# Softmax denominators of two attention pairs in one group of matrix products, in the first phase of a QK-norm attention and squared-ReLU kernel

## The chip, the cores and the metric

One core of one Trainium2 chip runs the whole program. The metric is device time in microseconds (us) from the first to the last instruction of the core with what lies around it; lower is better. All data are 32-bit floats. The engines are TensorE (PE, with its weight loads shown as PEld), VectorE (DVE), ScalarE (ACT), GpSimd (POOL) and SyncE (SP), which issues nearly all transfers.

## The reference

```
rmsnorm(x, g) = x / sqrt(mean(x*x) + 1e-6) * g
q_n, k_n = rmsnorm(q, g_q), rmsnorm(k, g_k)      # (8, 12, 448, 64): batch, heads, sequence, head size
attn = softmax(q_n @ k_n^T / sqrt(64))
a = attn @ v                                     # (8, 12, 448, 64)
x = a, heads side by side                        # (3584, 768)
out = relu(x @ w_in)^2 @ w_out                   # w_in 768 x 2048, w_out 2048 x 768
```

## The kernel before

Heads are worked on in *pairs*: pair `i` is two heads (`e` = 0, 1) of one batch, so 128 rows of "head element" on the partitions; there are 8 x 6 = 48. The 448 keys of a head are three blocks of 128 (`m` = 0, 1, 2) and 64 last ones (`m` = `NJ` = 3). The last keys of an even pair and of the odd pair behind it share one tile of 128 rows.

*Phase 1* is what the change touches: pairs 0 to 11 (`alone(i)`: the first two batches), before any of the second half's products exist to be mixed in. The instructions are in a hand-written order (a manual schedule): each engine works through its own in program order, and waits where data or a buffer isn't there. The loop makes 13 visits, each of two halves (`visit_alone(i, n)`). In visit `i`:

- `n = 0`: `weigh_slots` forms the scores of pair `i`, key blocks 0 and 1 (`score`: L449, 64x64 stationary tiles, four in different quarters of the array; PSUM banks 0 to 3), and ACT takes their exponentials (`weigh`, L468) into `weights`. `turn(i + 1, x)` transposes q (x = 0) and k (x = 1) of the next pair on PE (L415, L418; banks 7 and 6); DVE copies q and multiplies it by the gains (L423), ACT copies k (L425). `square(i + 2, x)` squares q on ACT (L181) and k on POOL (L183). `begin(step)` does pieces of a conversion of the second half's weights (ACT L1696 to L1699, DVE L1710, L1729, DVE or POOL L1810). `normalize(i + 2, 0)` sums the squares on DVE (L194, L197), raises them to -1/2 on POOL (L204), and scales q on POOL (L219). The factor for k goes into the exponential. Then `attend(i - 1)` multiplies the exponentials of the pair before by the values, blocks 0 to 2 (L552; `values_bank`: bank 4 for even pairs, 5 for odd ones).
- `n = 1`: scores and exponentials of block 2, in even visits also of the last keys of pairs `i` and `i + 1` (L460); `normalize(i + 2, 1)`; in odd visits `attend_both(i - 1)`, the last keys' values of two pairs (L588; the odd pair's part to bank 6, from where ACT copies it to `rest`, L595). Then for pair `i - 1`: `add_weights`, the denominators (L604): eight products of `ones` with the exponentials, each giving 32 equal rows in one of four column groups; `take_sums`, a DVE transpose in 32x32 blocks (L664); `invert`: four small copies (L675), an addition (L676), a reciprocal (L681) and a transpose that spreads the result again (L682); `finish`: DVE multiplies the values by the inverse (L717; for odd pairs after adding `rest`, L715). From the second batch on, `begin_forms` subtracts finished pairs from one another (L744): for its first three pairs one subtraction on DVE, for the last three one on DVE and two on POOL.

The buffers for `weights` are rooms in tiles named `part`, `acc` and `wT`.

After visit 12 the second half begins with L1016. It is mixed with the attention of the later pairs, whose denominators come in another way: POOL adds the exponentials up (L487), and one product for each head (L622) finishes the sum. For pair 12 that runs right behind phase 1.

The core of the order around the change:

```
            weigh_slots(i, n)
            turn(i + 1, 0)
            turn(i + 1, 1)
...
                attend(i - 1, (NJ,))
                add_weights(i - 1, range(NJ + 1))
                forget(i - 1, range(NJ + 1))
                take_sums(i - 1)
                invert(i - 1)
                finish(i - 1)
```

Of the kernel before, what the change touches and what calls it, by code (L numbers as in the profile page):

```python
# [14 lines left out]
F32 = mybir.dt.float32  # L15
# [4 lines left out]
ALU = mybir.AluOpType  # L20
# [3 lines left out]
P = 128  # L24


NJ = 3
NG = 2 * NJ + 1
SIDE = 32
# [196 lines left out]
def program(ctx, tc, rows, v, g, wide, ones, moe_w_in, moe_w_out, out, shift):  # L226

    nc = tc.nc

    B, H, S, D = v.shape  # L230
    NPAIR = H // 2
# [6 lines left out]
    NT = S // P  # L238
# [23 lines left out]
    banks = [psum.tile([P, 512], F32, name=f"bank{n}") for n in range(8)]  # L262
# [36 lines left out]
    def key_of(i, m):  # L299
        return (i - i % 2, m) if m == NJ and not shift else (i, m)  # L300

    def alone(i):

        return pairs[i][0] < 2
# [104 lines left out]
    def turn(i, x):  # L409

        ensure("qk", i)
        tr = banks[7 - x if i < 2 or alone(i - 2) else 0]
        dst = att.tile([P, S], F32, name="qT" if x == 0 else "kT")
        for j in range(NJ):
            nc.tensor.transpose(  # L415
                tr[:, ts(j, P)], rows.part(i, x)[:, j].rearrange("p h d -> p (h d)"), ident
            )
        nc.tensor.transpose(  # L418
            tr[:, ts(NJ, P)], rows.room(i)[:, x, NJ].rearrange("p h d -> p (h d)"),
            wide[:, ds(i % 2 * LASTS, P)],  # L420
        )
        if x == 0:
            nc.vector.tensor_scalar(out=dst, in0=tr[:, 0:S], scalar1=g, scalar2=None, op0=ALU.mult)  # L423
        else:
            nc.scalar.copy(dst, tr[:, 0:S])  # L425
        turned[i, x] = dst

    def new_weights(n, e):

        i, m = n  # L430
        if m < 2 and alone(i) and not shift:
            weights[n, e] = new_acc()[:, 0:S] if m else new_part()
        else:
            weights[n, e] = att.tile([P, S], F32, name="wT", tag="wT", bufs=8)
        return weights[n, e]

    def banks_of(i, m):

# [90 lines left out]
    def values_bank(i):  # L529
        return banks[4 + i % 2 if alone(i) else 4][:, 0:S]  # L530

    def attend(i, some):

        order = values_of(i)
        for n in (i, i + 1 if i % 2 == 0 and not shift else i):
            ensure("v", n)
        for n in some:  # L540
            if n >= len(order):
                continue
            m = order[n]
            if m == NJ and not shift:
                attend_both(i)
                continue
            if joint(i):
                attend_halves(i, n)
                continue
            mine = ds(i % 2 * LASTS, LASTS) if m == NJ else ds(0, P)  # L550
            for e in range(2):
                nc.tensor.matmul(  # L552
                    values_bank(i)[ds(e * D, D), :],
                    lhsT=lasts[i % 2][mine, e, :] if m == NJ else values[i][:, m, e, :],
                    rhs=weights[key_of(i, m), e][mine], start=n == 0,
                    stop=n == len(order) - 1 and (shift or i % 2 == 1),
                )

    def second_bank(i):
        return banks[3][:, 0:S]  # L560
# [36 lines left out]
    def add_weights(i, some):  # L597

        order = sums_of(i)
        for n in some:  # L600
            m = order[n]
            mine = ds(i % 2 * LASTS, LASTS) if m == NJ and shift else ds(0, P)
            for e in range(2):
                nc.tensor.matmul(  # L604
                    sums_bank(i)[ds(e * D + n % 2 * SIDE, SIDE), :],
                    lhsT=ones_of[i % 2][mine] if m == NJ else ones[:, 0:SIDE],
                    rhs=weights[key_of(i, m), e][mine], start=n < 2, stop=n >= 2,
                )
# [53 lines left out]
    def take_sums(i):  # L662
        inverse[i] = io.tile([P, S], F32, name="inverse", tag="squares", bufs=1)
        nc.vector.transpose(inverse[i], sums_bank(i))  # L664
# [4 lines left out]
    def invert(i):  # L669
        columns = inverse[i].rearrange("p (t n) -> p t n", n=SIDE)  # L670
        few = columns[:, :, 0:1]
        if alone(i) or shift:
            other, both = new_few(), new_few()
            for n in range(P // SIDE):
                nc.vector.tensor_copy(out=other[ts(n, SIDE)], in_=few[ts(n ^ 1, SIDE)])  # L675
            nc.vector.tensor_tensor(out=both, in0=few, in1=other, op=ALU.add)  # L676
            few = both
        if shift:
            nc.vector.tensor_scalar(out=few, in0=few, scalar1=1e-9, scalar2=None, op0=ALU.add)
        by = new_few()  # L680
        nc.vector.reciprocal(out=by, in_=few)  # L681
        nc.vector.transpose(columns, by.to_broadcast([P, S // SIDE, SIDE]))  # L682
# [22 lines left out]
    def finish(i):  # L705

        b, c = pairs[i]
        if joint(i):
            xT = xts[b, c]
            nc.gpsimd.tensor_tensor(out=xT, in0=xT, in1=inverse.pop(i), op=ALU.mult)  # L710
        else:
            xT = xts[b, c] = new_x()
            bank = values_bank(i)
            if i % 2 and not shift:
                nc.vector.tensor_tensor(out=xT, in0=bank, in1=rests.pop(i), op=ALU.add)  # L715
                bank = xT
            nc.vector.tensor_tensor(out=xT, in0=bank, in1=inverse.pop(i), op=ALU.mult)  # L717
        leave(i)

    def leave(i):  # L720
        b, c = pairs[i]
        scale_turned()
        for x in range(2):
            del turned[i, x]
        del values[i]
        if b == 1:
            begin_forms(c)
        elif b > 1:
            settle(b, c)
# [1129 lines left out]
    load_weights(1)  # L1859
    for i in range(2, 4):  # L1860
        rows.load(i, nc.sync)
    for n in range(2):
        nc.gpsimd.memset(ones_of[n][ds((1 - n) * LASTS, LASTS)], 0.0)
        nc.gpsimd.memset(ones_of[n][ds(n * LASTS, LASTS)], 1.0)

# [83 lines left out]
    def new_acc():  # L1949
        return keep_p.tile([P, DM], F32, name="acc", tag="acc", bufs=2 * NT + 1)  # L1950
# [30 lines left out]
    def visit_alone(i, n):  # L1981
        step = i * 2 * VISITS + 2 * n
        if n == 0:
            if i == 0:
                load_v(i)
            if i and shift:
                attend_all(i - 1)
            weigh_slots(i, n)
            turn(i + 1, 0)
            turn(i + 1, 1)  # L1990
            square(i + 2, 0, new_acc())
            square(i + 2, 1, new_acc(), nc.gpsimd)
            begin(step)
            normalize(i + 2, 0)
            if i and not shift:
                attend(i - 1, range(NJ))
        else:
            weigh_slots(i, n)
            normalize(i + 2, 1)
            begin(step)  # L2000
            if in_blocks(i + 2):
                store_q(i + 2)
                load_blocks(i + 2, 0)
                load_blocks(i + 2, 1)
            if i and not shift:
                attend(i - 1, (NJ,))
                add_weights(i - 1, range(NJ + 1))
                forget(i - 1, range(NJ + 1))
                take_sums(i - 1)
                invert(i - 1)  # L2010
                finish(i - 1)
            if i < 2 * NPAIR:
# [196 lines left out]
```

## Time and profile before

| | |
|---|---|
| runs | 1348.09, 1348.0, 1348.48; median 1348.09 us |
| profiled execution | 1348.26 us, its span 1346.5 us |
| granted TensorE clock | 0.999 |
| busy, share of the span | PE 98%, PEld 66%, DVE 66%, ACT 45%, POOL 56% |
| the profile's stretch of phase 1 | some 0 to 122 us |

The profile is one execution. "Busy" counts the time in which an engine works at something; matrix products are pipelined, so a busy PE can still be a PE that gains from fewer products. Each product of 32-bit floats stands as two instructions in the trace, so the eight products of a pair's denominators are L604 x16. Rows give line, engine, operation, tiles written and read, and shapes; a bracket at the end tells how long the engine stood idle before and what released it. The chain of waits follows the work that ended last back to its releasers.

### The profile page before, as it was taken

To read this page: it belongs to the slowest core of one execution; us is meant where nothing else is said; L and a number is where in the kernel's file an instruction comes from. 1 tells how busy PE (TensorE), PEld (TensorE's weight loads), DVE (VectorE), ACT (ScalarE), POOL (GpSimd) and SP (SyncE) were. 2 spreads that over 40 slices of the span, in tenths; PEclk is the share of its full clock that TensorE was granted. 3 is DMA by queue.
4 is the path that set the end of the run, shared out by engine and by line. 5 is a ranking of instruction groups with operands and counts; after the bars stand their busy time and mean duration, and the time that the engine had idled before them with its cause. 6 is when DMAs were issued, how large, how long until landed. Compare 5 with 4: busy or idle time off the path is not lost.

```text
span 1346.5 us, 21086 instructions
## 1 busy us (share of the span) xinstructions
PE 1326.0 (98%) x6988; PEld 887.2 (66%) x6988; DVE 884.0 (66%) x1739; ACT 611.4 (45%) x1135; POOL 760.6 (56%) x740
## 2 busy tenths in 40 slices
PE   7999999999999999999999999999999999999998
PEld 3333454444444486777758576676858599999998
DVE  4887866878768856465656856565655854556673
ACT  6885677768666244442434244353433134330000
POOL 5668764746556878566767878576555731110010
PEclk9999999999999999999999999999999999999999
DMA  5655965968969877574748676674737466545543
GB/s 137 156 142 131 247 187 144 283 182 219 266 149 268 255 189 221 154 219 124 234 104 251 190 186 211 169 214 119 238 83 231 145 194 196 157 132 152 161 158 101
DMA packets 416633, 245.64 MB, mean 182 GB/s; under 512 B 273284, under 2 KB 381060, under 8 KB 415492
## 3 DMA queue, kind: packets, MB, share of 16 engines
q1 hardware_dynamic: 416224, 244.15, 64.2%
q8 instruction: 57, 0.93, 0.3%
q14 instruction: 60, 0.49, 0.1%
q10 hardware_dynamic: 292, 0.07, 0.0%
HBM read 178.13 MB, written 65.99 MB: 181 GB/s over the span
## 4 chain that ended last, share of the span: by engine, by line
PE 90%; DVE 4%; DMA 2%; SPq 1%; POOL 1%; issue 1%; ACT 1%; POOLq 0%; DVEq 0%; ACTq 0%
PE bank L1077 26%; PE bank L1274 21%; PE bank L1600 9%; PE bank L1016 8%; PE bank L449 8%; PE bank L567 4%; PE bank L552 4%; PE bank L1438 2%; PE bank L460 1%; PE bank L588 1%; PE bank L604 1%; PE bank L1216 1%; PE bank L631 1%; PE bank L622 1%; DVE acc L1636 1%
## 5 line engine op out<-in xcount | busy, mean ns | idle before, releaser
L1077 PE MATMUL bank<-xT,in_sb 128*128 128x224 f32 x1344 | 287.0, 353 | 0.0
L1077 PEld LDWEIGHTS bank<-xT,in_sb 128*128 128x128 f32 x1344 | 253.1, 190 | 9.4 <-ACT wT L468 5.6
L468 ACT ACTIVATE wT<-bank,rr 128x448 f32<-128x448 f32 x288 | 163.8, 631 | 160.5 <-PE bank L449 134.9
L1274 PE MATMUL bank<-out_sb,hid 128*128 128x384 f32 x576 | 206.0, 490 | 1.7 <-DVE acc L1636 1.6
L204 POOL TENSOR_TENSOR rr<-ms,minus_half 128x8 f32<-128x8 f32 (+1 forms) x96 | 145.9, 1520 | 75.4 <-DVE ms L197 70.4
L1636 DVE TENSOR_TENSOR acc<-acc,bank 128x384 f32<-128x384 f32 x231 | 122.3, 546 | 78.7 <-PE bank L1274 58.6
L1274 PEld LDWEIGHTS bank<-out_sb,hid 128*128 128x128 f32 x576 | 107.7, 190 | 81.6 <-issue 6.6
L1274 PE MATMUL bank<-out_sb,sums 128*128 128x384 f32 x432 | 155.7, 491 | 1.1 <-DVE acc L1636 0.6
L449 PE MATMUL bank<-qT,kT 64*64 64x448 f32 x1152 | 147.0, 553 | 1.9 <-DVE qT L423 1.1
L1016 PE MATMUL bank<-xT,in_sb 128*128 128x448 f32 x336 | 129.8, 543 | 0.0
L1274 PEld LDWEIGHTS bank<-out_sb,sums 128*128 128x128 f32 x432 | 80.5, 190 | 65.5 <-issue 4.2
L487 POOL TENSOR_TENSOR sum<-sum,wT 128x448 f32<-128x448 f32 (+1 forms) x96 | 116.4, 1233 | 1.6
L1016 PEld LDWEIGHTS bank<-xT,in_sb 128*128 128x128 f32 x336 | 62.8, 190 | 66.8 <-issue 63.0
L1060 DVE TENSOR_TENSOR hid<-hid,bank 128x224 f32<-128x224 f32 x208 | 73.4, 382 | 44.3 <-PE bank L1077 41.1
L449 PEld LDWEIGHTS bank<-qT,kT 64*64 64x64 f32 x1152 | 49.5, 134 | 76.2 <-issue 50.8
L487 POOL TENSOR_TENSOR sum<-wT 128x448 f32<-128x448 f32 x48 | 56.1, 1189 | 73.1 <-ACT wT L468 66.5
L1077 PE MATMUL bank<-more,in_sb 128*128 128x224 f32 x288 | 74.4, 354 | 0.0
L567 PE MATMUL bank<-wT,vt 64*64 64x448 f32 x576 | 74.4, 545 | 0.0
L382 ACT ACTIVATE qT<-qT,g 128x448 f32<-128x448 f32 x34 | 22.5, 663 | 106.6 <-DVE qT L372 106.6
L1699 ACT ACTIVATE words<-words 128x384 f16<-128x384 f32 x64 | 68.6, 1072 | 2.0
L1547 POOL TENSOR_TENSOR acc<-acc 128x768 f32<-128x768 f32 x2 | 4.3, 2138 | 105.3 <-DVE acc L1519 105.3
L1060 DVE TENSOR_TENSOR whole_hid<-whole_hid,bank 128x224 f32<-128x224 f32 x104 | 37.7, 385 | 39.1 <-PE bank L1077 37.1
(200 smaller groups left out, 2374.7 us busy)
## 6 DMA issues: line engine op xcount, KB each, us to landing
in_sb<-in_deep SPq DMA_DIRECT2D x64, 384.0 KB, 3.8
in_sb<-in_deep SPq DMA_DIRECT2D x80, 256.0 KB, 4.3
out_sb<-out_forms SPq DMA_DIRECT2D x48, 384.0 KB, 5.6
words<-in_moe_w_in_dram SPq DMA_DIRECT2D x32, 384.0 KB, 3.9
words<-in_moe_w_out_dram SPq DMA_DIRECT2D x32, 384.0 KB, 3.5
out_forms<-out_sb SPq DMA_DIRECT2D x8, 1536.0 KB, 7.0
qk<-in_q_dram SPq DMA_DIRECT2D x96, 96.0 KB, 2.6
qk<-in_k_dram SPq DMA_DIRECT2D x96, 96.0 KB, 2.7
```

The lines of the kernel that those rows point to most:

```text
L204: self.nc.gpsimd.tensor_tensor(out=self.rr[i][:, x, 0 : self.count(i)], in0=ms, in1=self.minus_half.to_broadcast(list(ms.shape)), op=ALU.pow,)
L449: nc.tensor.matmul(sc[ds(half * D, D)], lhsT=turned[i, 1][ds(e * D, D), ds(m * P + half * D, D)], rhs=turned[i, 0][ds(e * D, D), :], start ...
L468: nc.scalar.activation(new_weights((i, m), e), sc, AF.Exp, scale=rows.rr[i][:, 1, 2 * m + e : 2 * m + e + 1],)
L487: nc.gpsimd.tensor_tensor(out=sums[i, e][some], in0=left[some], in1=weights[key_of(i, m), e][some], op=ALU.add)
L567: nc.tensor.matmul(bank[ds(e * D, D), :], lhsT=values[i][keys, n, e, :], rhs=weights[(i, n), e][keys], start=n == 0, stop=n == NJ - 1 and ...
L1016: nc.tensor.matmul(ps, lhsT=w_sb[:, IN.index(left), c, :], rhs=forms[u, c][right], start=first and c == 0, stop=c == NK - 1, skip_group_ch ...
L1060: nc.vector.tensor_tensor(out=quarter(blk, name, n), in0=quarter(blk, base, n), in1=ps, op=ALU.add)
L1077: nc.tensor.matmul(ps, lhsT=left, rhs=right, start=start, stop=stop, skip_group_check=True)
L1274: nc.tensor.matmul(ps, lhsT=lefts[left][:, t, ts(tt, P)], rhs=w_sb[t][:, OUT.index(right), :], start=first and t == 0, stop=t == 1, skip_g ...
L1600: nc.tensor.matmul(ps, lhsT=left[l][:, blk], rhs=rest_of[r][:, blk], start=blk == 0 and product in ("P1", "P5", "P4"), stop=blk == NBLK - ...
L1636: nc.vector.tensor_tensor(out=acc, in0=acc, in1=ps, op=ALU.add)
L1699: nc.scalar.activation(sign, high.bitcast(F32), AF.Copy)
```

## The change

- *Denominators of two pairs in one group.* Odd visits no longer form any. In even visits (2, 4, ... 12) `sums_of_two(i - 2)` forms those of pairs `i - 2` and `i - 1`: six products for each pair, with a stationary operand whose ones stand in 16 of 32 columns (the first 16 for the even pair, the other 16 for the odd one), and two for the shared last keys, each split in two products of 224 columns so that all four column groups work. All go to bank 6.
- *Inversion.* One transpose out of the bank, four small copies, an addition and a reciprocal serve both pairs (`invert_two`); two transposes spread the results.
- *Values.* In odd visits `leave_bank(i - 1)` copies the even pair's values from bank 4 to its `xT`, and `finish` later multiplies them there. In even visits both pairs are finished, one after the other.
- *Order of the turn.* In odd visits from 3 on, `turn(i + 1, 1)`, then `turn(i + 1, 0)`, stand ahead of the scores; k's transposes then use bank 4 instead of 6.
- *Rooms.* Exponentials live longer, so some go to tiles of the second half that are unused in phase 1 (`new_spare`); the masks with 16 columns of ones lie there too.

```
+    def turned_first(i):
+        return i % 2 == 0 and 2 < i <= 2 * NPAIR and not shift
...
-        tr = banks[7 - x if i < 2 or alone(i - 2) else 0]
+        tr = banks[4 if x and turned_first(i) else 7 - x if i < 2 or alone(i - 2) else 0]
...
+    def new_spare():
...
+        half = SIDE // 2
+        masks = more[:, 6 * S // SIDE : 6 * S // SIDE + 5 * half]
+        nc.gpsimd.memset(masks, 0.0)
+        nc.gpsimd.memset(masks[:, ts(1, half)], 1.0)
+        for n in range(2):
+            nc.gpsimd.memset(masks[ds(n * LASTS, LASTS), ts(3 + n, half)], 1.0)
+        spare.append([masks[:, ds(n * half, SIDE)] for n in (1, 0, 3)])
+
+    def room_for_weights(i, m, e):
+        if i % 4 == 0 or i == 2 * NPAIR - 1:
+            return spare[2 * m + e]
+        if m == 0:
+            return new_part()
+        if i % 2 == 0:
+            return spare[4 + 2 * m + e]
+        if m == 1:
+            return new_acc()[:, 0:S]
+        return att.tile([P, S], F32, name="wT", tag="wT", bufs=8)
...
+    def sums_of_two(i):
+        bank = banks[6][:, 0:S]
+        ones_for = spare[14]
+        for n in range(2 * NJ + 1):
+            p, m = divmod(n, NJ) if n < 2 * NJ else (0, NJ)
+            for e in range(2):
+                some = weights.pop(((i + p, m), e))
+                if m < NJ:
+                    nc.tensor.matmul(
+                        bank[ds(e * D + n % 2 * SIDE, SIDE), :], lhsT=ones_for[p], rhs=some,
+                        start=n < 2, stop=False, skip_group_check=True,
+                    )
+                    continue
+                for half in range(2):
+                    columns = ts(half, S // 2)
+                    nc.tensor.matmul(
+                        bank[ds(e * D + half * SIDE, SIDE), columns], lhsT=ones_for[2],
+                        rhs=some[:, columns], start=False, stop=True, skip_group_check=True,
+                    )
+        inverse[i] = io.tile([P, S], F32, name="inverse", tag="squares", bufs=1)
+        nc.vector.transpose(inverse[i], bank)
+        inverse[i + 1] = spare[10]
+
+    def invert_two(i):
+        columns = [inverse[i + p].rearrange("p (t n) -> p t n", n=SIDE) for p in range(2)]
+        few = columns[0][:, :, 0 : SIDE : SIDE // 2]
+        other, both, by = spare[11:14]
+        for n in range(P // SIDE):
+            nc.vector.tensor_copy(out=other[ts(n, SIDE)], in_=few[ts(n ^ 1, SIDE)])
+        nc.vector.tensor_tensor(out=both, in0=few, in1=other, op=ALU.add)
+        nc.vector.reciprocal(out=by, in_=both)
+        for p in range(2):
+            nc.vector.transpose(
+                columns[p], by[:, :, p : p + 1].to_broadcast([P, S // SIDE, SIDE])
+            )
+
+    def leave_bank(i):
+        xT = xts[pairs[i]] = new_x()
+        nc.vector.tensor_copy(out=xT, in_=values_bank(i))
+        del values[i]
...
+        elif (b, c) in xts:
+            xT = xts[b, c]
+            nc.vector.tensor_tensor(out=xT, in0=xT, in1=inverse.pop(i), op=ALU.mult)
...
-            weigh_slots(i, n)
-            turn(i + 1, 0)
-            turn(i + 1, 1)
+            if turned_first(i + 1):
+                turn(i + 1, 1)
+                turn(i + 1, 0)
+                weigh_slots(i, n)
+            else:
+                weigh_slots(i, n)
+                turn(i + 1, 0)
+                turn(i + 1, 1)
...
-            if i and not shift:
+            if i % 2 and not shift:
                 attend(i - 1, (NJ,))
-                add_weights(i - 1, range(NJ + 1))
-                forget(i - 1, range(NJ + 1))
-                take_sums(i - 1)
-                invert(i - 1)
+                leave_bank(i - 1)
+            elif i and not shift:
+                sums_of_two(i - 2)
+                invert_two(i - 2)
+                finish(i - 2)
                 finish(i - 1)
```

More of the change, by code (lines that the diff above doesn't have):

```diff
@@ L430, in new_weights @@
         i, m = n
-        if m < 2 and alone(i) and not shift:
-            weights[n, e] = new_acc()[:, 0:S] if m else new_part()
+        if m < NJ and alone(i) and not shift:
+            weights[n, e] = room_for_weights(i, m, e)
+        elif m == 1 and i == 2 * NPAIR and not shift:
+            weights[n, e] = new_acc()[:, 0:S]
         else:
@@ L435, in new_weights @@
         return weights[n, e]
+    spare = []
+    def new_spare():
+        for a in range(2):
+            some = hidden_p.tile([P, 2, 2, S], F32, name="hid", tag=f"hid{a}", bufs=1)
+            spare.extend(some[:, n // 2, n % 2] for n in range(4))
+        some = [
+            hidden_p.tile([P, 2, NT * P], F32, name="sums", tag=f"S{n}", bufs=1).rearrange(
+                "p t n -> p (t n)"
+            ) for n in range(3)
+        ]
+        spare.extend(x[:, 0:S] for x in some)
+        more = some[2][:, S : 2 * NT * P]
+        for n in range(3):
+            spare.append(more[:, ts(n, 2 * S // SIDE)].rearrange("p (t n) -> p t n", n=2))
+        half = SIDE // 2
[15 more added lines that the diff above has]
+        return att.tile([P, S], F32, name="wT", tag="wT", bufs=8)
     def banks_of(i, m):
@@ L724, in leave @@
             del turned[i, x]
-        del values[i]
+        values.pop(i, None)
         if b == 1:
@@ L1861, in program @@
         rows.load(i, nc.sync)
-    for n in range(2):
+    if not shift:
+        new_spare()
+    for n in range(2 if shift else 0):
         nc.gpsimd.memset(ones_of[n][ds((1 - n) * LASTS, LASTS)], 0.0)
@@ L2004, in visit_alone @@
                 load_blocks(i + 2, 1)
-            if i and not shift:
+            if i % 2 and not shift:
                 attend(i - 1, (NJ,))
-                add_weights(i - 1, range(NJ + 1))
-                forget(i - 1, range(NJ + 1))
-                take_sums(i - 1)
-                invert(i - 1)
+                leave_bank(i - 1)
[3 more added lines that the diff above has]
+                finish(i - 2)
                 finish(i - 1)
+                if i == 2 * NPAIR:
+                    spare.clear()
             if i < 2 * NPAIR:
```

## Prediction

> **What bounds the kernel now.** I read the page's totals first, then the chain of waits in order of time over phase 1 (the part that the change touches), then the timelines of PE, DVE, POOL and ACT over the same stretch, and last the busy time by pairs of visits.
>
> ```profile
> span 1346.5 us, 21086 instructions
> PE 1326.0 (98%) x6988; PEld 887.2 (66%) x6988; DVE 884.0 (66%) x1739; ACT 611.4 (45%) x1135; POOL 760.6 (56%) x740
> ```
>
> TensorE (PE) bounds the whole. Its share is an average, so phase 1 is read from its own chain. This is visit 3; columns are start, length, what:
>
> ```profile
> 36.56 1.66 PE bank L449 x16
> 38.22 0.48 PE bank L415 x3
> 38.70 0.11 PE bank L418
> 38.81 0.33 PE bank L415 x3
> 39.14 0.11 PE bank L418
> 39.25 2.40 PE bank L552 x12
> 41.65 0.91 PE bank L449 x8
> 42.56 0.75 PE bank L588 x8
> 43.32 1.64 PE bank L604 x16
> ```
>
> It ends at 44.96, 8.40 us without a gap: scores of key blocks 0 and 1 (1.66), the transposes of the next pair (0.48 + 0.11 + 0.33 + 0.11 = 1.03), the value products (2.40), scores of block 2 (0.91), the last keys (0.75; in even visits these are scores, L460), the denominators (1.64). L449 with 8 instructions takes 0.91 behind products of another shape; L588, also 8, takes 0.75 behind the same 64x64 shape. So a change of shape costs 0.16. Two visits, odd then even, take 16.8 while PE is the only limit. Here each window begins where an even visit's denominators end; the columns are length, then busy time of PE, PEld, DVE, ACT, POOL:
>
> ```profile
> 36.56:53.36 16.80, 16.80 (x140) 6.15 (x143) 14.73 (x37) 13.93 (x26) 9.69 (x8) 1.00 0.64 159
> 53.36:70.16 16.80, 16.80 (x140) 6.15 (x143) 14.25 (x34) 15.25 (x29) 10.50 (x9) 1.00 0.55 139
> 70.16:87.14 16.98, 16.98 (x140) 6.32 (x142) 15.76 (x38) 15.14 (x28) 11.99 (x11) 1.00 0.62 146
> 87.14:103.87 16.73, 16.73 (x137) 6.24 (x136) 14.59 (x35) 13.82 (x25) 8.78 (x8) 1.00 0.52 121
> 103.87:122.29 18.42, 17.01 (x141) 6.22 (x137) 15.97 (x33) 8.69 (x17) 15.85 (x14) 1.00 0.61 177
> ```
>
> Together 85.73. DVE is busy for 85 to 94% of the first four windows. It isn't the bound by its sum, but it works in program order, and one loop through it comes close. The denominators reach DVE, which inverts and divides; only behind that in its queue stand the qT copy of the next pair and the row sums (L194) of the pair after that; POOL raises those to a power (L204) and scales q by them (L219); the next visit's transposes need the scaled q. Visit 5, DVE and then POOL:
>
> ```profile
> 53.45 0.65 DVE L664 STREAM_TRANSPOSE inverse<-bank 128x448 f32<-128x448 f32 x1
> 54.13 1.67 DVE L675 COPY few<-inverse 32x14 f32<-32x14 f32 x4
> ...
> 56.32 0.65 DVE L682 STREAM_TRANSPOSE inverse<-few 128x448 f32<-128x448 f32 x1
> ...
> 57.51 0.77 DVE L717 TENSOR_TENSOR xT<-xT,inverse 128x448 f32<-128x448 f32 x1
> 58.20 0.67 DVE L423 TENSOR_SCALAR qT<-bank,g 128x448 f32<-128x448 f32 x1
> 58.80 0.54 DVE L194 TENSOR_REDUCE ms<-acc 128x6 f32<-128x384 f32 x1
> ...
> 59.62 1.36 POOL L204 TENSOR_TENSOR rr<-ms,minus_half 128x6 f32<-128x6 f32 x1 [1.83 <-DVE ms L197]
> 61.06 0.83 POOL L219 TENSOR_TENSOR qk<-qk,rr 128x384 f32<-128x384 f32 x1
> ```
>
> The loop ends at 61.89, 8.53 after the denominators (53.36). The transposes want it at 53.36 + 8.40 + 1.66 = 63.42. The other four odd visits, and the place where it fails already:
>
> ```profile
> 44.80 0.83 POOL L219 TENSOR_TENSOR qk<-qk,rr 128x384 f32<-128x384 f32 x1
> ...
> 79.00 0.95 POOL L219 TENSOR_TENSOR qk<-qk,rr 128x384 f32<-128x384 f32 x1
> ...
> 94.44 0.83 POOL L219 TENSOR_TENSOR qk<-qk,rr 128x384 f32<-128x384 f32 x1
> ...
> 114.60 0.83 POOL L219 TENSOR_TENSOR qk<-qk,rr 128x384 f32<-128x384 f32 x1
> 115.49 0.55 PE L415 MATMUL bank<-wide,qk 128*128 128x128 f32 x3 [0.96 <-POOL qk L219]
> ```
>
> Counted from the window's start, the loop ends at 9.07, 8.53, 9.79, 8.13 and 11.56, against a need at 10.06. It has 0.27 to 1.93 to spare, and in visit 12 PE stands 0.96 for it.
>
> **The change, part by part.** *Denominators.* Two groups (3.28) in two visits become one. Twelve products are as wide as now: 24 instructions, four at a time in four column groups, so 6 waves; a wave now takes (1.64 - 0.16)/4 = 0.37. Four products are half as wide. Their price is bounded by the full wave (0.37) and by half of it; the nearest row is of 224 columns:
>
> ```profile
> L1077 PE MATMUL bank<-xT,in_sb 128*128 128x224 f32 x1344 | 287.0, 353 | 0.0
> ```
>
> 287.0/1344 = 0.21, so a half wave is near 0.2; two of them. 6 x 0.37 + 0.4 + 0.16 = 2.76 (3.1 at the upper bound). Saved: 0.52 in two visits. Odd visits now end in 64x64 products and the next begins with such: one change of shape less, 0.16.
>
> *Order of the turn.* In odd visits transposes stand before the scores instead of behind them: the same shapes in turn, no PE time. k goes first, q second, so q is wanted 0.59 into the visit. Its loop started in an even visit, whose predecessor no longer inverts anything, so it is early: nothing. No transfer moves (q and k are loaded two visits ahead; the turn issues none). ACT's kT copy passes ahead of four exponentials which wait for later scores anyway: nothing.
>
> *No denominators in odd visits.* They covered the exponentials of block 2, which empty banks 0 and 1 before the next visit's scores write them. An odd visit is now 1.03 + 1.66 + 2.40 + 0.91 + 0.75 = 6.75. The exponentials end like this (visit 3):
>
> ```profile
> 42.60 1.16 ACT L468 ACTIVATE wT<-bank,rr 128x448 f32<-128x448 f32 x2
> ```
>
> 43.76 is 7.20 into the window: the new wait is 0.45, up to 1.0 where ACT converts words first, 0 where it doesn't. I take 0.5.
>
> *DVE.* One inversion for two pairs drops four copies, an addition, a reciprocal, and one 0.65 transpose out of a bank in two visits; a copy of the even pair's bank to xT is added in odd visits (L717's 0.6 as its price), where DVE waits for PE before its next transpose anyway. What counts is order: an even visit's denominators are now followed by both inverse transposes and both finishes. The stretch ahead of qT and L194 grows by one L682 (0.65) and one multiplication (0.6): 1.25. Behind visit 8's group one more subtraction for the forms joins it, behind visit 10's too; these rows are its price, and the late start of DVE in visit 10 as it is now:
>
> ```profile
> L744 DVE TENSOR_TENSOR xT<-xT x6: 624/624/626, 83.2 to 127.0; 128x448 f32<-128x448 f32 x6
> 105.02 0.64 DVE L664 STREAM_TRANSPOSE inverse<-bank 128x448 f32<-128x448 f32 x1
> ```
>
> *Sum.* From the end of one group to the next, PE's own order reaches the even visit's transposes at 6.75 + 0.5 + 1.49 = 8.74 (scores without a change of shape) and needs 1.03 + 2.40 + 1.66 + 2.76 = 7.85 from there. The loop ends later than now by 1.25 (visits 3, 5, 7), by 1.87 (visit 9, with that subtraction) and by 0.87 in visit 11: 1.87, less the 1.0 by which DVE, short of time there, starts late today (105.02 instead of 0.15 behind PE's 103.87) and will not with less to do. So it ends at 10.32, 9.78, 11.04, 10.00, 12.43, always beyond 8.74: PE stands for 1.0 to 3.7 in front of the transposes (qT of the odd pair, copied behind them, is wanted only 2.40 + 0.91 later). With 7.85 each the periods are 18.17, 17.63, 18.89, 17.85, 20.28, together 92.82: 7.1 more than 85.73. The bounds are no stand at all (16.59 x 5 = 82.95, a gain of 2.8) and some 2 more each, if POOL holds DVE up as below.
>
> *Visits 1 and 2.* Visit 1 drops 1.64 and a change of shape, visit 2 gains 1.12, and the bank waits (0.5, and some 0.35 until ACT has emptied bank 6 for the second transpose) take the rest: -0.7 to +0.3, I take 0.
>
> *End of phase 1.* Pair 10's forms (two subtractions on POOL) move one visit on, to those of pair 11. POOL and the chain there:
>
> ```profile
> 127.09 2.69 POOL L744 TENSOR_TENSOR xT<-xT 128x448 f32<-128x448 f32 x2 [1.21 <-DVE xT L717]
> 129.74 2.21 POOL L487 TENSOR_TENSOR sum<-wT 128x448 f32<-128x448 f32 x2
> 131.92 5.28 POOL L487 TENSOR_TENSOR sum<-sum,wT 128x448 f32<-128x448 f32 x4
> 137.28 0.94 PE bank L622 x4
> ```
>
> POOL's sums end at 137.20 and L622, which multiplies them, begins at 137.28: no slack. Four subtractions of 1.33 begin behind the first finish (about 127.0, as now: the second transpose and a multiplication stand where an addition and a multiplication do), so the sums start at 132.3, 2.6 later. I take 2.4 for L622; the bounds are 0 and 2.6. The squared-ReLU stage's first products use other forms and don't wait. The four memsets (0.12 each) are replaced by as many: nothing.
>
> 7.1 + 0 + 2.4 = 9.5. The profiled execution took 1348.26 (span 1346.5 and 1.8 around it), 0.17 over the median of 1348.09, so I forecast 1348.1 + 9.5 = **1357.6**: slower by 0.7%. After phase 1 PE is dense, so nothing gives it back.
>
> **Rivals.** *B, faster:* the odd pairs' q is scaled by the time it is wanted, and the change gives what it saves on PE. This decides at 8.74 into the window. Then 82.95 for five periods, 2.8 less, or 5.3 less without bank waits; with POOL's sums in time 1342.8 to 1345.3, else near 1347.7. For it: DVE has some 1.5 less to do in two visits (the four copies, the transpose, two small ones, less the new copy). Against: it has idle time already, and the loop starts at the denominators, whatever DVE had free before them. Chance 0.12.
>
> *C, about the same:* the stands are short. Four L675 copies take 1.67 in visit 5, and this is DVE waiting: in visit 9 the same four take 0.72, as the next row has it.
>
> ```profile
> 87.95 0.72 DVE L675 COPY few<-inverse 32x14 f32<-32x14 f32 x4
> ```
>
> If POOL is quiet at these moments, the loops end 0.9 earlier and five periods take 88.3, 2.6 more; with POOL's last sums hidden, 1350.7. Chance 0.18.
>
> *D, much slower:* DVE and POOL hold each other up more. An addition out of SBUF that takes 0.18 elsewhere took 0.82 beside a POOL operation, and ended with it:
>
> ```profile
> 38.15 0.82 DVE L676 TENSOR_TENSOR few<-inverse,few 128x14 f32<-128x14 f32 x1
> 38.12 0.83 POOL L183 TENSOR_TENSOR acc<-qk 128x384 f32<-128x384 f32 x1
> ```
>
> The even pairs' multiplication, which read a bank and one operand in SBUF, now reads both from SBUF. A wait of 0.64 to 0.9 in each window, there and in the copies, makes 3 to 4.5 more: 1360.6 to 1362.1. Half-wide products that don't go four at a time would also end here. Chance 0.08. [...]
>
> **How the numbers follow.** The forecast has 0.62, and 1351 to 1361 as its own range. A change of 0.2% (2.7) is about what a measurement of this kernel can tell from none. Slower by more: 0.62 + 0.08 + 0.07 of C = 0.77. Within: 0.11 of C and 0.03 of B = 0.14. Faster: 0.09 of B. The range 1346.5 to 1362.0 leaves out the faster part of B (0.09) and the outermost of the others (some 0.08).
>
> **What would show it.** Right: in even visits L415 waits for POOL qk L219 by 1 to 3.7 each; the group of denominators takes near 2.8, once in two visits; the next scores wait some 0.5 for ACT; DVE idles in odd visits before the next group; L622 waits for POOL's sum. Wrong: these transposes begin straight behind the scores; DVE's row sums come before the finishes; or L622 doesn't wait. If the periods come out near 16.6, the loop isn't as long as I made it.

## Result, and the profile after

| | before | after |
|---|---|---|
| median of 5 runs | 1348.09 us (1347.8 to 1348.48) | 1361.44 us (1360.99 to 1363.24) |
| profiled execution, its span | 1348.26, 1346.5 | 1360.99, 1358.7 |

The ratio is 1.0102, with an interval of 1.0087 to 1.0117: slower by 1%. The forecast was 1357.6, in a range of 1346.5 to 1362.0. The page's totals after the change:

```profile
span 1358.7 us, 21033 instructions
PE 1329.4 (98%) x6988; PEld 889.6 (65%) x6988; DVE 871.9 (64%) x1703; ACT 612.3 (45%) x1135; POOL 761.8 (56%) x740
```

DVE has 12.1 us less to do than before, and the span is 12.2 longer: what counts here is where the work stands, not how much there is. The changed kernel's visits 3 to 12 in pairs, each window from the end of one group of denominators to the end of the next; columns as in the prediction (length, busy time of PE, PEld, DVE, ACT, POOL, then the granted clock):

```profile
35.83:54.11 18.28, 16.97 (x141) 6.59 (x138) 14.07 (x31) 14.84 (x28) 11.59 (x10) 1.00 0.65 162
54.11:71.35 17.24, 16.92 (x138) 6.60 (x138) 11.20 (x27) 15.81 (x29) 11.36 (x11) 1.00 0.58 151
71.35:91.83 20.48, 18.57 (x137) 7.21 (x138) 13.27 (x31) 14.55 (x26) 12.51 (x11) 0.92 0.45 106
91.83:109.79 17.96, 16.89 (x137) 6.57 (x137) 14.50 (x32) 13.90 (x25) 8.37 (x7) 1.00 0.57 142
109.79:129.23 19.44, 16.62 (x137) 6.78 (x137) 11.61 (x25) 10.22 (x19) 13.85 (x12) 1.00 0.48 145
```

Together 93.40 against 85.73: +7.67. A window's length less PE's busy time is what PE stands still. Here are these stands, from PE's timeline: the transposes of the even visits (L419, before: L415), with the idle time before them in brackets, and who ended it. (Some 0.3 more in each window but the third is a wait ahead of the scores.)

```profile
46.18 0.55 PE L419 MATMUL bank<-wide,qk 128*128 128x128 f32 x3 [0.98 <-POOL qk L219]
82.19 0.55 PE L419 MATMUL bank<-wide,qk 128*128 128x128 f32 x3 [1.91 <-POOL qk L219]
101.79 0.55 PE L419 MATMUL bank<-wide,qk 128*128 128x128 f32 x3 [0.72 <-POOL qk L219]
121.20 0.55 PE L419 MATMUL bank<-wide,qk 128*128 128x128 f32 x3 [2.48 <-POOL qk L219]
```

Only visit 6 has none. The loop that ends one of them (visit 3 into 4), on DVE and then POOL:

```profile
35.97 0.65 DVE L622 STREAM_TRANSPOSE inverse<-bank 128x448 f32<-128x448 f32 x1 [2.00 <-PE bank L617]
36.66 1.33 DVE L631 COPY sums<-inverse 32x28 f32<-32x28 f32 x4
...
39.72 0.58 DVE L799 TENSOR_TENSOR xT<-xT,inverse 128x448 f32<-128x448 f32 x1
40.22 0.62 DVE L804 TENSOR_TENSOR xT<-bank,rest 128x448 f32<-128x448 f32 x1
40.87 0.62 DVE L806 TENSOR_TENSOR xT<-xT,sums 128x448 f32<-128x448 f32 x1
41.41 0.68 DVE L427 TENSOR_SCALAR qT<-bank,g 128x448 f32<-128x448 f32 x1
...
42.97 0.55 DVE L194 TENSOR_REDUCE ms<-acc 128x6 f32<-128x384 f32 x1
...
43.80 1.42 POOL L204 TENSOR_TENSOR rr<-ms,minus_half 128x6 f32<-128x6 f32 x1 [6.23 <-DVE ms L197]
45.30 0.83 POOL L219 TENSOR_TENSOR qk<-qk,rr 128x384 f32<-128x384 f32 x1
```

POOL stands idle for 6.23 us and waits for a row sum (L194) of 0.55 that itself needs nothing from the finishes (L799 to L806) in front of it; PE's transposes wait for POOL. The longest stand, that of visit 12, has one more link. There the finishes also release two subtractions for the forms on POOL, and these and k's squares (L183, 0.84) stand ahead of the power in POOL's own order, so that the row sum (done at 118.20) waits in turn:

```profile
115.50 2.68 POOL L833 TENSOR_TENSOR xT<-xT 128x448 f32<-128x448 f32 x2 [3.99 <-DVE xT L806]
...
118.91 1.33 POOL L204 TENSOR_TENSOR rr<-ms,minus_half 128x6 f32<-128x6 f32 x1
```

The rest of the difference lies at the end of phase 1, on POOL and then on PE (L708 multiplies POOL's last sums, as L622 before):

```profile
133.09 6.09 POOL L833 TENSOR_TENSOR xT<-xT 128x448 f32<-128x448 f32 x4 [4.34 <-DVE xT L799]
139.14 2.79 POOL L529 TENSOR_TENSOR sum<-wT,acc 128x448 f32<-128x448 f32 x2
141.88 5.82 POOL L529 TENSOR_TENSOR sum<-sum,wT 128x448 f32<-128x448 f32 x4
129.06 4.78 PE L1105 MATMUL bank<-xT,in_sb 128*128 128x448 f32 x12
146.55 0.96 PE L708 MATMUL bank<-sum,ones 128*64 128x448 f32 x2 [2.42 <-POOL sum L529]
147.76 1.01 PE L708 MATMUL bank<-sum,ones 128*64 128x448 f32 x1 [0.25 <-POOL sum L529]
152.60 1.77 PE L1105 MATMUL bank<-xT,in_sb 128*128 128x448 f32 x4
```

The same two marks in the kernel before:

```profile
122.22 4.78 PE L1016 MATMUL bank<-xT,in_sb 128*128 128x448 f32 x12
140.57 1.77 PE L1016 MATMUL bank<-xT,in_sb 128*128 128x448 f32 x4
```

From the second half's first product to the point where its products go on: 18.35 before, 23.54 after, +5.19. Up to visit 2 the change gains 0.73 (the first window begins at 35.83 instead of 36.56). -0.73 + 7.67 + 5.19 = 12.1, the 12.2 of the spans. The profiled executions differ by 12.73, the medians by 13.35. Of that, 0.5 is time around the span (1.8 before, 2.3 after), which no view explains; the profiled execution is the shortest of the five after.

*The clock.* Two of the stands cost more than they last. PE alone, in stretches of 2 us from about the end of the stand of visit 8 (82.19); columns are length, busy time, granted clock:

```profile
82.00:84.00 2.00, 1.81 (x10) 0.68 0.67 152
84.00:86.00 2.00, 2.00 (x8) 0.50 0.88 221
86.00:88.00 2.00, 2.00 (x16) 0.97 0.00 2
```

In slices of 0.4 us the clock reads 1.00 up to 82.40, then 0.89, 0.50 from 82.80 to 86.00, 0.85, and 1.00 again from 86.40: at half for some 3.4 us. (0.32 + 0.50 + 0.03) x 2 = 1.7 us lost. The same happens behind the stand of 2.42 at the end of phase 1 (0.89, 0.50 and 0.76 in the stretches of 2 us from 146.00, again 1.7), and not behind that of 2.48 in visit 12, whose window shows 1.00.

### The profile page after: what moved, and what is told of

Read it like the earlier page. It is cut to its first block, busy times and chain, and to the rows that moved or that the text cites. A ratio compares the mean times of both kernels' runs of the same rounds, so it can differ in the third digit from the quotient of the medians.

```text
span 1358.7 us, 21033 instructions
## 1 busy us (share of the span) xinstructions
PE 1329.4 (98%) x6988; PEld 889.6 (65%) x6988; DVE 871.9 (64%) x1703; ACT 612.3 (45%) x1135; POOL 761.8 (56%) x740
## 4 chain that ended last, share of the span: by engine, by line
PE 84%; DVE 5%; issue 3%; POOL 3%; DMA 2%; SPq 2%; ACT 1%; POOLq 0%; DVEq 0%; ACTq 0%
PE bank L1166 26%; PE bank L1363 20%; PE bank L1689 9%; PE bank L1105 7%; PE bank L491 7%; PE bank L653 4%; PE bank L594 3%; PE bank L1527 2%; PE bank L502 1%; PE bank L674 1%; PE bank L717 1%; DMA qk<-in_k_dram 1%; DMA out_forms<-out_sb 1%; PE bank L1305 1%; PE bank L708 1%
## 5 line engine op out<-in xcount | busy, mean ns | idle before, releaser
L510 ACT ACTIVATE wT<-bank,rr 128x448 f32<-128x448 f32 x272 | 155.6, 632 | 154.7 <-PE bank L491 131.3
L491 PE MATMUL bank<-qT,kT 64*64 64x448 f32 x1152 | 149.7, 552 | 3.2 <-ACT wT L510 1.8
L491 PEld LDWEIGHTS bank<-qT,kT 64*64 64x64 f32 x1152 | 51.3, 133 | 75.8 <-issue 48.3
```

The source lines that it names most:

```text
L491: nc.tensor.matmul(sc[ds(half * D, D)], lhsT=turned[i, 1][ds(e * D, D), ds(m * P + half * D, D)], rhs=turned[i, 0][ds(e * D, D), :], start ...
L510: nc.scalar.activation(new_weights((i, m), e), sc, AF.Exp, scale=rows.rr[i][:, 1, 2 * m + e : 2 * m + e + 1],)
```

## Experiments

The theory: the even visits' transposes wait for a loop (denominators, inversion, both finishes, row sums, POOL) in which the two finishes are queued ahead of the row sums; and POOL's last sums are late by the two subtractions that moved. Rivals: PE's own work and waits for banks set the periods; or the new order of the turn is what costs. Edits are against the changed kernel unless it says otherwise. Ratios are against runs of the kernel before taken beside each experiment: their medians are 1347.61 for experiments 1 to 4, 1347.8 for 5 to 8 and 1348.28 for 9 and 10.

**1. The finishes behind the row sums.**

```
             normalize(i + 2, 0)
+            if i % 2 and i > 1 and not shift:
+                finish(i - 3)
+                finish(i - 2)
...
                 invert_two(i - 2)
-                finish(i - 2)
-                finish(i - 1)
                 if i == 2 * NPAIR:
+                    finish(i - 2)
+                    finish(i - 1)
```

> The changed kernel, with the two finishes of an even visit (three DVE operations of 0.5 to 0.6 each, and the subtractions for the forms) moved behind the next odd visit's first row sums on DVE. Theory (the loop from the denominators through DVE's queue and POOL to the odd pair's scaled q makes PE stand): the loop ends 1.7 us earlier, 2.9 where forms are subtracted, so near 8.6, 7.9, 9.1, 8.2 and 7.5 behind the group, and PE, which reaches the transposes 9.3 behind it, doesn't stand; five periods of some 17.2 instead of 18.3, 17.2, 20.5, 18.0, 19.4: 7.4 less, 1354.0. Rival (DVE and POOL hold each other up, the order in the queue matters little): 1359.5 to 1361.5. Rival (PE's own new order is longer than reckoned): no change, 1361.4.

Measured: 1352.52 (1352.3 to 1353.6), ratio 1.0038 [1.0024, 1.0052]. The first of its five windows, PE alone, and what is left of PE's waits (engine and line, for what: total, times, longest):

```profile
35.50:52.70 17.20, 16.88 (x144) 1.00 0.71 177
```
```profile
PE bank L708 <- POOL sum L529: 2.8, 2, 2.5
...
PE bank L419 <- POOL qk L219: 1.2, 2, 0.7
```

The five periods (35.50 to 121.40) take 85.90 instead of 93.40. The finishes, moved by a few places in the queues with nothing taken away, were worth 7.5 us, of which 1.7 is the half clock of visit 8. They are two multiplications and an addition on DVE; in visits 10 and 12 the subtractions for the forms go with them, on POOL too, so for visit 12 the edit doesn't tell DVE's share from POOL's. The remaining 4.9 above before is about the end of phase 1, which this edit leaves alone (23.73 here, +5.38).

**2. POOL's sums ahead of the moved subtractions.**

```
-        less(nc.gpsimd, some["T3"], b22, some["T3"])()
-        less(nc.gpsimd, t4, t2, b21)()
+        behind.append(less(nc.gpsimd, some["T3"], b22, some["T3"]))
+        behind.append(less(nc.gpsimd, t4, t2, b21))
...
                 additions(i)
+                pool_tasks.extend(behind)
```

> The changed kernel, with POOL's four subtractions for the forms of pairs 10 and 11 put behind its six additions for pair 12's denominators. Theory (these additions come 3 us late, PE stands for them, and its clock drops behind that): the product of the sums starts without a wait, as before the change; the 5.1 us of the end of phase 1 go, 1356.3. If only the stand goes and the lower clock stays: 1358. Rival (DVE, behind two finishes, is late for the second half's first products in any case): 1360 or more.

Measured: 1358.87 (1357.3 to 1359.38), ratio 1.0083 [1.0066, 1.01]: 2.6 less than the changed kernel instead of 5. The end of phase 1, from PE's timeline:

```profile
140.79 7.03 PE L1110 MATMUL bank<-xT,in_sb 128*128 128x448 f32 x18 [0.84 <-DVE xT L804]
147.75 0.97 PE L708 MATMUL bank<-sum,ones 128*64 128x448 f32 x4
```

L708 no longer waits, and this stretch takes 19.22 (131.85 to 151.07) against 23.54. So 4.3 came back here, less than 5.2 because a new wait of 0.84 turned up: a product that goes to bank 5 waits until L804 has emptied it, and L804 is late. What made it late is not shown here; in experiment 7, where POOL's additions come first too, the last inversion's four copies took 2.60 beside them, against 0.76 in the changed kernel. But in this execution the clock fell in visit 12 too:

```profile
110.41:131.35 20.94, 18.12 (x140) 7.64 (x136) 11.60 (x25) 10.22 (x19) 14.95 (x13) 0.92 0.47 140
```

20.94 instead of 19.44 gives 1.5 back. The subtractions are confirmed as the cause at the end; the total also depends on which stands the clock answers, and that isn't the same in two executions: the stand of visit 12 is 2.48 here and in the changed kernel, which kept its clock (1.00).

**3. More work for PE just ahead of the even visits' transposes**, two 64x64 products that nothing reads.

```
                 weigh_slots(i, n)
+                if i % 2 == 0 and i > 2 and not shift:
+                    for half in range(2):
+                        nc.tensor.matmul(banks[7][ds(half * D, D), 0:S], ...)
```

> The changed kernel, with two additional 64x64 products of 448 columns (0.75 us of PE) in front of the transposes of visits 4, 6, 8, 10 and 12; they write a bank that the transposes overwrite, so nothing else changes. Theory (PE stands there for 1.0, 0, 1.9, 0.7 and 2.5 us, waiting for the scaled q): only visit 6 pays, +0.75, and where the stand of visit 8 no longer lets the clock drop, 1.7 less: 1360.4 to 1362.2. Rival (PE's own work sets the periods): 5 x 0.75 = 3.7 more, 1365.1.

Measured: 1362.43 (1359.3 to 1363.84), ratio 1.0112 [1.0093, 1.0131], beside 1.0102 without them. The products turned out shorter than the 0.75 reckoned: PE's busy time in the five periods grew by 1.4 in all (87.38 against 85.97). The times scatter too much to tell that from nothing, but the windows can: the five periods took 93.60 (35.92 to 129.52) against 93.40, with one stretch of half clock in either. The stands shrink instead (0.98, 1.91, 0.72, 2.48 become 0.71, 1.69, 0.45, 1.90):

```profile
119.99 0.55 PE L419 MATMUL bank<-wide,qk 128*128 128x128 f32 x3 [1.90 <-POOL qk L219]
```

So PE's own arrival doesn't set these periods; the loop does. In this execution the slow stretch stood behind the stand of 1.90 (the twelve value products there, L594, took 3.72, against 2.48 in the changed kernel's visit 12 at a clock of 1.00), not behind that of 1.69 (1.00 from 78.00 to 88.00).

**4. The turn behind the scores again.** `turned_first` returns `False`.

> The changed kernel, with the transposes behind the scores in odd visits too, as before the change (k's transposes in bank 6 again). Theory: the order of the two costs PE nothing and the loop through DVE is the same: 1361.4, within 1. Rival (transposes in front expose the exponentials of the scores behind them): faster by 2 or more, 1359 or less. Rival (transposes behind wait for bank 6, which holds the denominators): slower by 1 or more.

Measured: 1362.36 (1360.95 to 1363.25), ratio 1.0109 [1.0092, 1.0126]. In its profile PE stands for the scaled q by 1.32, 0.24, 2.26, 1.04 and 2.48. The five periods took 95.34 (36.61 to 131.95), 1.9 more than the changed kernel's; 1.7 of it is the half clock, which here stood behind the stand of visit 12 (the twelve value products took 3.20, against 2.48) as well as that of visit 8 (0.69 and 0.50 in the two stretches of 2 us from 84.00). Without it the order of the turn is worth nothing that can be told, as the prediction had it.

**5. The loop in the kernel before.** If the loop is the cause, and not the denominators themselves, the kernel before must lose time too when only DVE is held up in this place. Three needless operations of 0.6 each behind the finish of the odd pairs, against the kernel before:

```
             nc.vector.tensor_tensor(out=xT, in0=bank, in1=inverse.pop(i), op=ALU.mult)
+            if i % 2 and i < 2 * NPAIR - 2 and not shift:
+                for _ in range(3):
+                    nc.vector.tensor_tensor(out=xT, in0=xT, in1=xT, op=ALU.max)
```

> The kernel before, with three additional DVE operations of 0.6 behind the finish of each odd pair from 1 to 9 (the maximum of the result with itself), so 1.9 us more ahead of the next visit's row sums, and nothing else. Theory (a loop from the denominators through DVE and POOL to the scaled q, with 1.0, 1.5, 0.3, 1.9 and no time to spare): PE stands 0.9, 0.4, 1.6, 0 and 1.9 more in the even visits, 4.8, and 1.7 more for each time that the clock drops: 1352.5 to 1355. Rival (DVE has room for it, as its busy share of some 90% in phase 1 says): within 1 of the kernel before.

Measured: 1354.8 (1353.86 to 1354.87), ratio 1.005 [1.0035, 1.0066], +7.0. PE's largest wait is the one of the changed kernel, and the clock falls behind the longest stand (PE alone: length, busy time, clock):

```profile
PE bank L415 <- POOL qk L219: 7.1, 6, 2.6
```
```profile
118.00:121.00 3.00, 0.47 (x8) 1.00 0.80 180
121.00:124.00 3.00, 2.89 (x14) 0.66 0.11 25
```

The added work is 9 us in five pairs of visits, in which DVE had 10.4 idle (85.73 less the 75.3 of its busy time): there was room for it, but not ahead of the row sums.

**6. Edits 1 and 2 together.**

> The changed kernel with both moves: the finishes behind the next odd visit's first row sums, and POOL's last four subtractions behind its additions. Theory: the two causes add up; from the 5 us by which the first move alone stayed behind the kernel before go the 4.4 of the end of phase 1 (0.8 stay: the third product of the second half waits for bank 5): within 1 of the kernel before, 1347 to 1349. If something else stays hidden behind these two: 1350 or more.

Measured: 1350.48 (10 runs, 1348.82 to 1351.47), ratio 1.0017 [1.0008, 1.0027]. This recovers 11 of the 13 us. The five periods (35.85 to 121.89) take 86.04, and the wait for bank 5 is there:

```profile
131.15 7.03 PE L1110 MATMUL bank<-xT,in_sb 128*128 128x448 f32 x18 [1.16 <-DVE xT L804]
```

The profiled execution is the shortest of the ten, with a span of 1346.6, that of before. The 1.7 by which the median lies above it has no profile.

**7. Block 2 of the odd visits in banks 2 and 3**, so that the next scores don't wait for ACT (added to edit 6).

```
+        if m == NJ - 1 and i % 2 and alone(i) and not shift:
+            return [banks[2 + e][:, 0:S] for e in range(2)]
         return [banks[m % 2 * 2 + e][:, 0:S] for e in range(2)]
```

> The kernel with both moves, and the scores of key block 2 in odd visits in banks 2 and 3 instead of 0 and 1. Theory (the scores of the next even visit wait 0.3 for the exponentials of block 2 and then run in two halves that don't overlap, 2.24 instead of 1.49): its first half now finds banks 0 and 1 free and the second has 0.75 more; 0.4 to 0.6 less in each of six pairs of visits, 2.4 to 3.6 in all, where the loop to the scaled q (some 8 us) doesn't take a part back: 2 to 3.5 less than with both moves, so 2 or 3 faster than the kernel before. Rival (PE is held by ACT's sequence, not by these banks): as with both moves.

Measured: 1350.99 (1350.39 to 1351.86), ratio 1.0025 [1.0015, 1.0035]. A miss: no gain. The wait went away, and the five periods fell to 84.49, but others took its place:

```profile
PE bank L419 <- POOL qk L219: 2.5, 4, 1.6
PE bank L1112 <- DVE xT L806: 2.3, 1, 2.3
```

The sooner PE arrives, the longer it waits for POOL; and the product for bank 5 now waits for 2.3. On DVE the subtraction ahead of the addition that empties the bank took 2.53 there (128.42 to 130.95), at first beside POOL's additions (until 129.37); the same subtraction took 0.62 in the changed kernel (L833 at 133.04).

**8. The inversion too behind the row sums** (`invert_two` goes along with the finishes; added to edit 7).

> As the kernel with block 2 elsewhere, but the inversion (transposes, copies, reciprocal) stands behind the odd visit's first row sums as well, not the finishes alone. Theory: the row sums then wait for ACT's squares (4.7 behind the group) rather than for DVE, so the loop ends near 7.8, a few tenths earlier: the stand of visit 8 (0.5) goes, else the same: within 0.7 of the kernel with block 2 elsewhere, rather faster. Rival (the inversion, now late, holds bank 5 for the next values): slower by 1 to 3.

Measured: 1353.0 (1351.88 to 1354.62), ratio 1.0043 [1.0029, 1.0057], 2 worse, also a miss. A row of its waits and one from ACT's timeline tell why:

```profile
PE bank L419 <- ACT rest L683: 5.8, 6, 1.6
...
117.85 0.53 ACT L683 COPY rest<-bank 128x448 f32<-128x448 f32 x1 [2.66 <-DVE xT L806]
```

ACT's copy of the odd pair's last values into `rest` (L683) waits until the finish of the odd pair before it (L806 here) has read that tile, which is now later, and the bank that ACT empties is the one that the transposes of k want.

**9. Bank 5 left early** (edit 6, and the odd pair's values and `rest` are added before the denominators).

```
+        if i % 2:
+            nc.vector.tensor_tensor(out=xT, in0=values_bank(i), in1=rests.pop(i), op=ALU.add)
+        else:
             nc.vector.tensor_copy(out=xT, in_=values_bank(i))
...
+                leave_bank(i - 1)
                 sums_of_two(i - 2)
```

> The kernel with both moves, and the odd pair's addition (its values in bank 5 and the rest, 0.6 on DVE) put ahead of the denominators instead of behind the inversion, since it needs no inverse. Theory: DVE idles there, so it costs nothing; bank 5 is free in time for the second half's third product (1.2 less), and the row sums of block 2's k and what stands behind them come 0.6 earlier: 1.2 to 2 less than with both moves, 1348.5 to 1349.3. Rival (DVE then holds PE up in front of the denominators, or other waits take the place): no gain.

Measured: 1349.02 (11 runs, 1347.87 to 1350.44), ratio 1.0006 [0.9997, 1.0015]. No different from before.

**10. Edits 7 and 9, and in even visits k turned first, in bank 7, q in bank 6**, so that q, which is wanted late, comes second.

```
+        if i % 2 and 2 < i < 2 * NPAIR + 2 and not shift:
+            tr = banks[6 + x]
...
+                for x in (1, 0) if i % 2 == 0 and i > 1 and not shift else (0, 1):
+                    turn(i + 1, x)
```

> As the kernel whose odd values leave early, with block 2 of odd visits in banks 2 and 3, and in even visits k turned ahead of q, k in bank 7 and q in bank 6. Theory (with block 2 elsewhere PE reaches the transposes 0.9 earlier and there stands 0.8 for ACT's copy out of bank 6 and up to 1.6 for the scaled q): either has 0.55 more time, the end of phase 1 doesn't wait, and of the 6 x 0.5 that the banks give most stays: 2.5 to 4 less than with block 2 elsewhere alone, 1347 to 1348.5, so the same as the kernel before or 1 faster. Rival (ACT's sequence bounds phase 1 by now): 1349 or more.

Measured: 1346.2 (11 runs, 1344.72 to 1347.77) beside 1348.28 of before, ratio 0.9983 [0.9974, 0.9992]: faster than both kernels, by 0.17%. Its five periods:

```profile
35.44:119.05 83.61, 82.57 (x684) 32.57 (x680) 67.02 (x146) 68.12 (x125) 58.03 (x47) 1.00 0.61 157
```

83.61 is 2.1 less than before's 85.73. That is a gain, but less than the prediction had for PE without stands: 2.8 (82.95) with 0.5 a period for the banks in it, 5.3 without these waits, which edit 7 removes. 1.04 is still lost in stands. Most of the rest is not idle time: the even visits' scores take up to 1.9 instead of 1.49, and in one visit the last keys' scores 1.4 instead of 0.75.

## Why the prediction was right, and where its steps were off

The direction and the cause were right: DVE's order, not its sum, makes the even visits wait for POOL's q. Experiments 1, 3 and 5 show it from three sides. The size was off: 1361.44 lies just above the 1351 to 1361 that the forecast gave itself, and inside the 1360.6 to 1362.1 of rival D. Yet D's mechanism (DVE and POOL hold each other up more) was not the cause in the five periods: the even pairs' multiplication out of SBUF (L799) took 0.58 in each of the five windows, and no loop ended later than forecast; no window shows the some 2 more that the prediction allowed for it in each. What lifted the time is the clock and the end of phase 1, below. Rival B's condition (q scaled in time) was met only in visit 6, and only experiment 10 gave a gain, smaller than B's.

- *The group of denominators*, 2.76 forecast (its terms add up to 2.78). From the chain (start, length, what):

```profile
51.34 2.39 PE bank L610 x24
53.73 0.38 PE bank L617 x8
```

  2.77. The half-wide products do go four at a time: two waves in 0.38.
- *Loop ends*, 10.32, 9.78, 11.04, 10.00 and 12.43 forecast; measured 10.30, 8.64, 10.78, 9.91 and 11.36 behind the group. Two are 1.1 too late. I had taken over the small copies at the length they had before, 1.67 and 1.66 in visits 5 and 11. There rival C's argument held, and the four took 0.77 and 0.76. POOL wasn't idle, but it ran its power alone; before, it scaled and converted data at that moment (in visit 5 L219 for 1.04 and L1810 for 1.00, over the copies' 1.67). Visit 5 now:

```profile
54.87 0.77 DVE L631 COPY sums<-inverse 32x28 f32<-32x28 f32 x4
...
54.12 1.64 POOL L204 TENSOR_TENSOR rr<-ms,minus_half 128x8 f32<-128x8 f32 x1
```

- *The new wait for banks 0 and 1*, 0.5 forecast. Its price is about 1.0: in visit 6 the transposes come at 63.37, 9.26 behind the group, where 8.74 was forecast. PE stood 0.32, and then the scores ran in parts: behind the first four weight loads the others waited 0.33 more for ACT (PEld, L491 at 61.71), and the 16 took 2.24 instead of the 1.73 that an undisturbed row takes:

```profile
61.20 2.24 PE L491 MATMUL bank<-qT,kT 64*64 64x448 f32 x16 [0.32 <-ACT wT L510]
```

  In the other visits (loop end less stand) PE came 8.9 to 9.3 behind the group. Where it stands for the loop anyway this changes nothing; in visit 6 it set the period.
- *The periods*, 18.17, 17.63, 18.89, 17.85 and 20.28 forecast, 92.82 together; measured 18.28, 17.24, 20.48, 17.96 and 19.44, 93.40. The sum is close partly by luck: visit 8 has 1.7 that no step held (10.78 + 7.98 as in visit 4 = 18.76, and then the half clock), against 0.84 too much in visit 12.
- *Visits 1 and 2*, 0 forecast, -0.73 measured, just outside the bound of -0.7.
- *End of phase 1*: this term of the sum was mis-sized, +2.4 (bounds 0 to 2.6) against +5.19. The stand itself is 2.42 + 0.25, near what was forecast, though by another account: POOL began its subtractions sooner, took 6.09 for four instead of 5.3, and 8.61 for the sums instead of 7.49. The rest lies behind the stand: 1.7 by the half clock, and some 0.8 (5.19 less 2.67 less 1.7) that fits the products being released one by one; that is an estimate, and no run isolates it. Nothing in the working held a price for what follows a stand.
- *The turn's order* at nothing: shown by experiment 4.

Left out was the clock. Its price is 1.7 in visit 8 and 1.7 at the end; terms that were forecast too high (visits 1 and 2, visits 6 and 12) hid part of it. Result and forecast lie 3.8 apart: 2.7 in the span (12.2 against 9.5), 0.5 in the time around it, and 0.6 by which the medians lie further apart than the profiled executions. The last two stay open. So does why one stand is followed by the half clock and another isn't.

## What to carry to other kernels

When work is gathered into fewer, larger steps, look at what stands behind it in the queue of the engine that does it: a short operation that opens the next loop (here a row sum of 0.55) should go ahead of results that nobody waits for soon. Here each wait taken away handed the time to the next one, so a gain on the bounding engine arrived only when nearly all of them were gone (experiments 6 to 10). And a stand of about 2 us on TensorE should be priced with what the clock may add behind it: 1.7 in each of the two cases in the changed kernel.

## What was not expected of the hardware

- *Behind some stands of about 2 us TensorE's granted clock was 0.50 for some 3.4 us* (visit 8 of the changed kernel, 82.80 to 86.00 and the slices at either end), at a cost of 1.7. Shortest stand with it: 1.90 (experiment 3); longest with it: 2.65 (experiment 5, visit 12); longest without, from visit 3 on: 2.48 (the changed kernel, visit 12), and the same 2.48 had it in experiments 2 and 4. There it was present when that stand ended (the three transposes took 0.90 in both, against 0.55 in the changed kernel), and it set in some 1.5 behind the stand of 2.26 in experiment 4, which ended at 83.25 (1.00 up to 84.00, then 0.69 and 0.50 in stretches of 2 us).
- *Four small copies on DVE took more than three times as long beside POOL's additions.* Those that took 0.77 in visit 5 took 2.60 at the end of phase 1 in experiment 7, and the addition behind them 1.06 instead of 0.20, beside POOL's work:

```profile
122.06 2.60 DVE L633 COPY sums<-inverse 32x28 f32<-32x28 f32 x4
124.69 1.06 DVE L634 TENSOR_TENSOR sums<-inverse,sums 128x28 f32<-128x28 f32 x1
```
```profile
122.40 2.21 POOL L531 TENSOR_TENSOR sum<-wT,acc 128x448 f32<-128x448 f32 x2
124.57 4.80 POOL L531 TENSOR_TENSOR sum<-sum,wT 128x448 f32<-128x448 f32 x4
```

  The copies end when POOL's two additions do (124.66 and 124.61). The addition reads two operands out of SBUF, as does the one of the prediction's rival D that took 0.82 beside POOL; the copies read one. What held either isn't shown.
